# Batch 0 of a retention and gated-MLP kernel: the order of work on four engines, written anew

## The chip, the cores and the metric

The kernel runs on one core of a Trainium2 chip. A core has a matmul engine (PE, with weight loads as PEld), a vector engine (DVE), a scalar engine (ACT), GpSimd (POOL), and SyncE (SP), which here only issues DMA transfers. Each engine works through its own list of instructions in order and waits at an instruction until the semaphores it names have come. The metric is the device time of one execution in microseconds (us); lower is better.

## The reference, cut to what matters

```
scores = scale * (q @ k.T)                      # per batch (8) and head (8), 576 x 576
ret    = scores * gamma[h] ** (i - j), i >= j   # decay mask
x      = ret @ v                                # 576 x 512 per batch
h      = relu(x @ w_in);  u, v = h[:, :512], h[:, 512:]
v_n    = (v - mean) / sqrt(var + 1e-6)
v_s    = w_spatial @ v_n + b_spatial
out    = (u * v_s) @ w_out
```

All of it is in float32, for 8 batches.

## The kernel before, in words

Every large product is made of three fp32r matmuls on operands split into a rounded part (hi) and a remainder (lo): `mm3`. So each operand has to be split first: ACT writes hi, then DVE or POOL writes lo.

The **retention** of a batch b goes over the sequence in chunks c = 0 to 4, four of 128 rows and a tail of 64 (`NC` = 4).

- `scores(b, c)` puts a chunk's score matmuls into one of two PSUM banks, r_95 and r_96 (the two alternate); DVE multiplies by the mask into the tile `at`.
- `prep(b, c)` lets POOL scale k by `kd` (tile `qkv`) and q by `qs` (tile `qsc`).
- `burst(b, c, nx)` does on PE, in one run, the state products (need the scaled k), the product with the old state (needs the scaled q), the scores of the next chunk if one is given, and the product with `at`. Then DVE adds up the state `st` and POOL decays it.
- `evac(b, c)` copies the result out of PSUM: ACT writes hi and DVE lo, into `x`, for the tail into `xt`. The next burst uses the same bank and waits for it.
- `load(b, c)` has SP fetch a chunk's qkv (1024 KB) and q (256 KB). The qkv tiles have two buffers, so a load waits for the burst two chunks back.

The **MLP** of a batch has stages. `v_steps(b, sb)` is one row block of v in steps: matmuls, ACT's relu, DVE's statistics, ACT's square root and subtraction, the reciprocal chain on DVE (tile `sm`) and the split into `vn` (tail: `vt1`, `vt2`). `vs_mm` is one tile of w_spatial @ v_n: 12 matmuls 128x288 on `wsp` and `vn`, then one with `wtl[0]` and one with `wtl[1]`. `u_mm` is a tile of u, f is the output product.

The **weights** come as 8-byte words of which the kernel makes float32. `front(kind, i)` takes the absolute value on ACT and clamps it on POOL (tile `f`), `mid` is a DVE TENSOR_SCALAR and two SCALAR_TENSOR_TENSOR, `back` is the split into `win` or `wout` (ACT, then POOL). Kind 1 is the v half of w_in, kind 0 its u half, kind 2 is w_out; `fetch` loads block i of one. `w_sp_steps` splits w_spatial: four blocks, and in its fifth step the tail `wtl` with the row of b_spatial.

The steady part, batches 1 to 7 from v1 on, is ordered by a scheduler. Batch 0 and the retention of batch 1 are ordered by hand: while `ordered[0]` is true, each engine issues in the order in which the program's text calls it. `go(gen, n)` does the next n steps of such a generator; `ret` is the retention of batch 1, whose first `go` does the scores of chunk 0 and whose later ones a burst with its evac and its next load each. PSUM for all but the retention is four buffers in turn (`ps_m`).

Since one helper issues every ordered instruction, all have line L71 in the profile; tiles tell them apart.

Of the kernel before, what the change touches and what calls it, by code (L numbers as in the profile page):

```python
# [33 lines left out]
def retention_gmlp(ctx, tc, qkv, q_x, qk_t, q_xt, v_t, w_in, w_sp, b_sp, w_out, amask, qscale, kdec, sdec, out):  # L34
# [20 lines left out]
    def slot(name):  # L55
        return cp.tile([P, 2, NCB, S], F32R, name=name, tag="slot", bufs=2)
# [24 lines left out]
    def dma(dst, src):  # L81
        return sy.dma_start(out=dst, in_=src)
# [88 lines left out]
    for i in range(2, NCB):  # L171
        fetch(1, i)
    dma(sd, sdec)
    load(0, 1)
    dma(qs, qscale)
    load(0, 2)
    load(0, 3)
    load_qsc(0, NC)
# [9 lines left out]
    def front(kind, i, clamp=po):  # L188
        words = staged[kind, i].rearrange("p (n two) -> p n two", two=2)
        hw, lw = words[:, :, 1], words[:, :, 0]  # L190
        f = early[:, i] if kind == 1 else sp.tile([P, 512], F32, name=f"f_{kind}{i}", tag="f", bufs=3)
        a = f if clamp is po else ps_m.tile([P, 512], F32, name=f"w_{kind}{i}", tag="m")
        ac.activation(out=a, in_=hw.bitcast(F32), func=AF.Abs)
        if clamp is po:
            po.tensor_scalar(out=a, in0=a, scalar1=2.0 ** -15, scalar2=None, op0=ALU.max)
        part[kind, i] = hw, lw, a, f
# [27 lines left out]
    def w_sp_steps():  # L224
        w = staged["s"]
        for sb in range(NC):
            split(wsp[0][:, sb], wsp[1][:, sb], w[:, sb], po)
            yield
        t = w[:, NC]
        ac.copy(out=wtl[0], in_=t)  # L230
        po.tensor_tensor(out=wtl[1][:TL], in0=t[:TL], in1=wtl[0][:TL].bitcast(F32), op=ALU.subtract)
        r = slice(TL, TL + 1)
        t = w[r, NC + 1]
        ac.copy(out=wtl[1][r], in_=t)
        po.tensor_tensor(out=wtl[1][96:97], in0=t, in1=wtl[1][r].bitcast(F32), op=ALU.subtract)
        yield

    xs = {}
# [82 lines left out]
            po.tensor_copy(out=xs[b][:, :, :, t], in_=xt.rearrange("p a i n -> p i a n"))  # L321

    def retention(b):
        xs[b] = slot(f"x_{b}")
        nxt = [(b, c) for c in range(NC + 1)] + [(b + 1, c) for c in range(2)]
        if (b, 0) not in at:
            prep(b, 0)
            scores(b, 0)
        yield 0.95
        for c in range(NC + 1):  # L330
            nx = nxt[c + 1] if nxt[c + 1][0] < B and (b, c) != (1, NC) else None
            if nx:
# [12 lines left out]
    def v_steps(b, sb):  # L345
        n = C if sb < NC else TL
        x = xs[b]
        pf = ps_m.tile([P, 512], F32, name=f"v_{b}_{sb}", tag="m")
        ps = pf[:n]
        t = slice(sb * C, sb * C + n)  # L350
        if sb < NC:
            for cb in range(NCB):
                if cb == 2 and (b, sb) == (0, 3):
                    yield
                mm3(ps, [x[:, i, cb, t] for i in range(2)], [win[i][:, cb, DH:] for i in range(2)], cb == 0, cb == NCB - 1)
        else:
# [12 lines left out]
        mv = wk.tile([P, 2], F32, name=f"mv_{b}_{sb}", tag="mv", bufs=3)[:n]
        ve.bn_aggr(out=mv, in_=s6)  # L370
        s = wk.tile([P, 5], F32, name=f"sm_{b}_{sb}", tag="sm", bufs=3)[:n]
        ac.activation(out=s[:, 0:1], in_=mv[:, 1:2], func=AF.Sqrt, bias=eps[:n])
        ac.activation(out=ps, in_=ps, func=AF.Identity, scale=-1.0, bias=mv[:, 0:1])
        yield
        r = s[:, 1:2]
        ve.reciprocal(out=r, in_=s[:, 0:1])
        ve.tensor_scalar(out=s[:, 2:3], in0=mv[:, 1:2], scalar1=EPS, scalar2=r, op0=ALU.add, op1=ALU.mult)
        ve.tensor_scalar(out=s[:, 3:4], in0=s[:, 2:3], scalar1=r, scalar2=0.5, op0=ALU.mult, op1=ALU.mult)
        ve.tensor_scalar(out=s[:, 4:5], in0=s[:, 3:4], scalar1=-1.5, scalar2=r, op0=ALU.add, op1=ALU.mult)
        nrstd = s[:, 4:5]  # L380
        if sb < NC:
            hi, lo = vn[0][:, sb], vn[1][:, sb]
        else:
            hi, lo = vt1[:TL], vt1[TL:]
            ac.activation(out=vt2[:TL], in_=ps, func=AF.Copy, scale=nrstd)
        ac.activation(out=hi, in_=ps, func=AF.Copy, scale=nrstd)
        yield
        ve.scalar_tensor_tensor(out=lo, in0=ps, scalar=nrstd, in1=hi.bitcast(F32), op0=ALU.mult, op1=ALU.subtract)
        yield
# [85 lines left out]
    def go(gen, n=1):  # L475
        for _ in range(n):
            next(gen)
# [9 lines left out]
    front(1, 2, ve)  # L487
    back(1, 1)
    front(1, 3)
    burst(0, 0, None)  # L490
    mid(1, 2)
    evac(0, 0)
    load(0, NC)
    fetch(0, 0)
# [2 lines left out]
    scores(0, 1)  # L497
    back(1, 2)
    mid(1, 3)
    burst(0, 1, None)  # L500
    back(1, 3, ve)
    fetch_wsp()
    evac(0, 1)
    load(1, 0)
    for i in range(1, NDB):
        fetch(0, i)
    prep(0, 2)
    scores(0, 2)
    vn = [cp.tile([P, NC, DH], F32R, name=f"vn{i}", tag=f"vn{i}") for i in range(2)]
    v = [v_steps(0, sb) for sb in range(NC + 1)]  # L510
    m = [mid_steps(0, i) for i in range(NDB)]
    sps = w_sp_steps()

    go(v[0], 2)
    burst(0, 2, None)
    go(v[0])
    front(0, 0)
    evac(0, 2)
    prep(0, 3)
    scores(0, 3)  # L520
    go(v[0], 2)
    go(v[1], 2)
    burst(0, 3, None)
    go(v[1])
    go(m[0])
    evac(0, 3)
    prep(0, NC)
    scores(0, NC)
    go(v[1], 2)
    go(m[0])  # L530
    go(v[2], 2)
    burst(0, NC, None)
    go(sps, 2)
    load(1, 1)
    go(v[2])
    evac(0, NC)
    back(0, 0)
    go(v[3])
    go(v[4])
    go(v[3])  # L540
    go(v[2], 2)
    go(v[4])
    go(v[3])
    go(sps)
# [2 lines left out]
    for t in range(2):  # L547
        ps = ps_m.tile([P, 512], F32, name=f"u_0_0_{t}", tag="m")[:, :HALF]
        u_mm(0, 0, t, ps)
        ac.activation(out=pre[:, t, :HALF], in_=ps, func=AF.Relu)  # L550
    go(v[4])
    go(v[3])
    go(sps)
    go(v[3])
    go(v[4])
    go(v[3])
    go(sps)
    go(v[4])
# [4 lines left out]
    def u_work():
        for i in range(1, NDB):
            front(0, i)
            yield
            go(m[i])
            yield
            go(m[i])
            back(0, i)  # L570
            yield

    def wout_work():
        for i in range(NMB):
            fetch(2, i)
        for i in range(NMB):
            front(2, i)
            yield
            mid(2, i)
            yield  # L580
            back(2, i)
            yield

    work = u_work()
    for t in range(2):
        ts = slice(t * HALF, (t + 1) * HALF)
        for db in range(NDB):
            ps = vs_mm(0, db, t)
            if db:
                ac.copy(out=u[:, db, ts], in_=ps)  # L590
            else:
                ve.tensor_tensor(out=u[:, db, ts], in0=ps, in1=pre[:, t, :HALF], op=ALU.mult)
            next(work, None)
            if (t, db) in ((0, 2), (1, 1)):
                go(ret)
            next(work, None)
    for _ in work:
        pass
    wout = [cp.tile([P, NDB, DM], F32R, name=f"wout{i}", tag=f"wout{i}") for i in range(2)]
    work = wout_work()  # L600
    g0 = xs[0]
    for t in range(2):
        ts = slice(t * HALF, (t + 1) * HALF)
        for db in range(1, NDB):
            ps = ps_m.tile([P, 512], F32, name=f"u_0_{db}_{t}", tag="m")[:, :HALF]
            u_mm(0, db, t, ps)
            ve.scalar_tensor_tensor(out=u[:, db, ts], in0=ps, scalar=0.0, in1=u[:, db, ts], op0=ALU.max, op1=ALU.mult)
            next(work)
            if db == 2:
                go(ret)  # L610
        split(g0[:, 0, :, ts], g0[:, 1, :, ts], u[:, :, ts], po)
    ordered[0] = False
    for eng in (pe, ve, ac, po):
        ctx.enter_context(tc.issue_after(eng.last))
# [85 lines left out]
```

## Time and profile before

| | us |
|---|---|
| time, median of 3 runs (range) | 570.96 (570.17 to 571.62) |
| the profiled execution: its own time | 569.64 |
| its span, first to last instruction | 567.9 |
| PE busy in the span | 539.2 |
| PE busy in 0 to 122 us | 96.43 |
| PE busy in 122 to 568 us | 442.74 |
| DVE, ACT, POOL busy in the span | 266.1, 207.2, 132.7 |

Batch 0's stages are the first 122 us. In a timeline row the columns are start, duration, engine, line, operation, output and inputs, shape, count, and in brackets the idle time ahead of the row with what ended it. Neighbouring rows of one kind are merged, so a duration can cover many instructions. In a row of a table by stretches stand the stretch, its length, the busy time (and count) of PE, PEld, DVE, ACT and POOL, the granted PE clock (1.00 is full), the DMA share and GB/s.

### The profile page before, as it was taken

To read this page: it belongs to the slowest core of one execution; us is meant where nothing else is said; L and a number is where in the kernel's file an instruction comes from. 1 tells how busy PE (TensorE), PEld (TensorE's weight loads), DVE (VectorE), ACT (ScalarE), POOL (GpSimd) and SP (SyncE) were. 2 spreads that over 40 slices of the span, in tenths; PEclk is the share of its full clock that TensorE was granted. 3 is DMA by queue.
4 is the path that set the end of the run, shared out by engine and by line. 5 is a ranking of instruction groups with operands and counts; after the bars stand their busy time and mean duration, and the time that the engine had idled before them with its cause. 6 is when DMAs were issued, how large, how long until landed. Compare 5 with 4: busy or idle time off the path is not lost.

```text
span 567.9 us, 15304 instructions
## 1 busy us (share of the span) xinstructions
PE 539.2 (95%) x6735; PEld 501.3 (88%) x6735; DVE 266.1 (47%) x588; ACT 207.2 (36%) x445; POOL 132.7 (23%) x131
## 2 busy tenths in 40 slices
PE   6885689899999999999999999999999999999997
PEld 5764689789999899998999899998999889998997
DVE  5855445480463473417353373516543383515340
ACT  4237221582212462226422362225522362225422
POOL 4635554670031220121201221021201212000000
PEclk8889789899999999999999999999999999999999
DMA  8972228301346421342224441342213432010002
GB/s 326 377 236 86 92 96 266 115 1 42 117 125 192 171 95 47 105 166 76 95 48 145 138 156 48 95 169 83 95 47 126 145 104 88 27 64 21 2 1 84
DMA packets 37045, 64.08 MB, mean 113 GB/s; under 512 B 14833, under 2 KB 27249, under 8 KB 33010
## 3 DMA queue, kind: packets, MB, share of 16 engines
q1 hardware_dynamic: 36978, 63.10, 33.7%
q8 instruction: 53, 0.87, 0.7%
q14 instruction: 14, 0.11, 0.1%
HBM read 53.65 MB, written 9.44 MB: 111 GB/s over the span
## 4 chain that ended last, share of the span: by engine, by line
PE 84%; POOL 5%; DVE 4%; DMA 3%; ACT 2%; issue 1%; SPq 0%; POOLq 0%; ACTq 0%; DVEq 0%
PE vs L71 20%; PE f L71 18%; PE u L71 17%; PE v L71 15%; PE r L71 14%; POOL f L71 2%; DVE f L71 2%; DMA qs<-in_qscale 2%; DMA am<-in_amask 1%; POOL x L71 1%; POOL qsc L71 1%; POOL qkv L71 1%; DVE st L71 1%; ACT x L71 1%; DVE at L71 0%
## 5 line engine op out<-in xcount | busy, mean ns | idle before, releaser
L71 PE MATMUL vs<-wsp,vn 128*128 128x288 f32 x768 | 114.1, 297 | 0.0
L71 PE MATMUL u<-x,win 128*128 128x288 f32 x768 | 106.6, 298 | 1.0 <-POOL f L71 1.0
L71 PEld LDWEIGHTS vs<-wsp,vn 128*128 128x128 f32 x768 | 105.2, 188 | 1.2
L71 PEld LDWEIGHTS u<-x,win 128*128 128x128 f32 x768 | 104.2, 190 | 2.3 <-POOL f L71 1.2
L71 PE MATMUL v<-win,x 128*128 128x512 f32 x384 | 94.1, 400 | 0.0
L71 PE MATMUL f<-g,wout 128*128 128x288 f32 x672 | 92.3, 296 | 0.0
L71 PEld LDWEIGHTS f<-g,wout 128*128 128x128 f32 x672 | 89.8, 188 | 0.5
L71 DVE TENSOR_TENSOR at<-r,am 128x1024 f32<-128x1024 f32 (+1 forms) x40 | 44.5, 1112 | 93.4 <-PE r L71 93.4
L71 PEld LDWEIGHTS v<-win,x 128*128 128x128 f32 x384 | 71.8, 190 | 16.8
L71 POOL TENSOR_TENSOR qsc<-qsc,qs 128x512 f32<-128x512 f32 (+1 forms) x31 | 36.3, 1171 | 175.8 <-DMA qsc<-in_q_x 99.6
L71 PEld LDWEIGHTS r<-qkv 64*64 64x64 f32 x2176 | 48.4, 141 | 25.8 <-POOL qkv L71 15.3
L71 PE MATMUL r<-qkv 64*64 64x64 f32 (+1 forms) x2176 | 54.9, 242 | 17.0 <-POOL qkv L71 13.1
L71 DVE BATCH_NORM_STATS2 s<-v 128x6 f32<-128x512 f32 (+1 forms) x40 | 27.8, 694 | 59.4 <-ACT v L71 58.4
L71 ACT COPY o<-f 128x288 f32<-128x288 f32 x64 | 25.6, 400 | 72.0 <-PE f L71 71.9
L71 ACT CAST g<-vs 128x288 fp32r<-128x288 f32 x56 | 22.3, 399 | 75.8 <-DVE vs L71 74.7
L71 POOL TENSOR_TENSOR qkv<-qkv,kd 128x512 f32<-128x512 f32 x32 | 33.3, 1044 | 41.6 <-DMA qkv<-in_qkv 27.3
L71 ACT CAST x<-r 128x512 fp32r<-128x512 f32 x32 | 18.7, 585 | 60.7 <-DVE st L71 60.7
L71 PE MATMUL r<-at,qkv 64*64 64x64 f32 (+1 forms) x1152 | 38.8, 232 | 0.0
L71 DVE TENSOR_TENSOR g<-vs,g 128x288 fp32r<-128x288 f32 x56 | 25.6, 457 | 26.3 <-ACT g L71 26.3
L71 DVE TENSOR_TENSOR vs<-vs,u 128x288 f32<-128x288 f32 x56 | 26.0, 464 | 23.1 <-PE vs L71 23.0
L71 PEld LDWEIGHTS r<-at,qkv 64*64 64x64 f32 (+1 forms) x1152 | 33.2, 145 | 2.5 <-DVE at L71 0.2
L71 POOL TENSOR_TENSOR st<-st,sd 128x256 f32<-128x256 f32 x24 | 14.7, 614 | 87.2 <-DVE st L71 87.2
(73 smaller groups left out, 504.5 us busy)
## 6 DMA issues: line engine op xcount, KB each, us to landing
qkv<-in_qkv SPq DMA_DIRECT2D x31, 1024.0 KB, 5.7
out<-o SPq DMA_DIRECT2D x64, 144.0 KB, 1.8
qsc<-in_q_x SPq DMA_DIRECT2D x24, 256.0 KB, 3.2
raw_v<-in_w_in SPq DMA_DIRECT2D x4, 512.0 KB, 6.3
qkv<-in_qk_t SPq DMA_DIRECT2D x8, 256.0 KB, 3.4
qkv<-in_v_t SPq DMA_DIRECT2D x16, 128.0 KB, 3.1
raw<-in_w_in SPq DMA_DIRECT2D x4, 512.0 KB, 8.6
raw<-in_w_out SPq DMA_DIRECT2D x4, 512.0 KB, 7.3
```

The costliest lines, as they stand in the source:

```text
L71: ins = op(*args, **kw)
```

## The change

Only text between the start of the kernel and the line `ordered[0] = False` is different. The stages come in the same order (v0, vs0, u0, v1, u1, f0), and the number of matmuls, casts and transfers is the same, except that the split of the gated result goes in halves (`split_g`, two ACT casts and two POOL subtractions for one each). The core of the diff:

```diff
+    dma(qs, qscale)
     load(0, 1)
-    dma(qs, qscale)
...
+    mid(1, 2)
     burst(0, 0, None)
-    mid(1, 2)
     evac(0, 0)
...
     mid(1, 3)
-    burst(0, 1, None)
     back(1, 3, ve)
     fetch_wsp()
+    burst(0, 1, None)
+    prep(0, 2)
     evac(0, 1)
...
-    go(v[0], 2)
+    go(v[0], 3)
+    prep(0, 3)
     burst(0, 2, None)
+    evac(0, 2)
     go(v[0])
     front(0, 0)
-    evac(0, 2)
-    prep(0, 3)
     scores(0, 3)
-    go(v[0], 2)
-    go(v[1], 2)
+    go(v[0])
+    go(v[1], 3)
+    prep(0, NC)
     burst(0, 3, None)
-    go(v[1])
     go(m[0])
     evac(0, 3)
-    prep(0, NC)
+    go(v[1])
     scores(0, NC)
-    go(v[1], 2)
-    go(m[0])
+    go(v[1])
+    go(sps, 2)
     go(v[2], 2)
     burst(0, NC, None)
-    go(sps, 2)
+    evac(0, NC)
+    go(v[2])
+    go(m[0])
+    back(0, 0)
     load(1, 1)
-    go(v[2])
-    evac(0, NC)
-    back(0, 0)
+    fetch(2, 0)
+    prep(1, 0)
+    go(sps)
     go(v[3])
     go(v[4])
     go(v[3])
     go(v[2], 2)
     go(v[4])
     go(v[3])
     go(sps)
+    ret = retention(1)
+    xs[1] = slot("x_1")
+    scores(1, 0)
+    go(v[4])
+    go(v[3])
+    go(sps)
...
         ac.activation(out=pre[:, t, :HALF], in_=ps, func=AF.Relu)
+        go(v[4 - t])
     go(v[4])
     go(v[3])
...
-    ret = retention(1)
-    go(ret)
     go(ret)
+    vs_tile(0, 0)
+    go(ret)
+    front(0, 1)
+    vs_tile(0, 1)
+    front(0, 2)
+    vs_tile(0, 2)
+    go(m[1], 2)
+    vs_tile(0, 3)
+    back(0, 1)
+    front(0, 3)
+    fetch(2, 1)
+    go(ret)
+    vs_tile(1, 0)
+    go(m[2], 2)
+    vs_tile(1, 1)
+    back(0, 2)
+    fetch(2, 2)
+    vs_tile(1, 2)
+    go(ret)
+    go(m[3], 2)
+    vs_tile(1, 3)
+    back(0, 3)
+    fetch(2, 3)
+    front(2, 0)
+    gated_u(0, 1)
+    gated_u(0, 2)
+    front(2, 1)
+    go(ret)
+    mid(2, 0)
+    gated_u(0, 3)
+    back(2, 0)
+    split_g(0)
+    gated_u(1, 1)
+    gated_u(1, 2)
+    go(ret)
+    mid(2, 1)
+    gated_u(1, 3)
+    back(2, 1)
+    split_g(1)
...
```

Left out at the dots are, above all, the old form of the lower half: six more steps of v[3], v[4] and sps ahead of the retention, and two loops that took the same vs and u tiles with `front`, `mid` and `back` of w_in's blocks 1 to 3 and of w_out one step after each tile. There all four `fetch(2, i)` stood together, between the vs tiles and the u tiles. `vs_tile`, `gated_u` and `split_g` are the bodies of those loops, given names.

In the last step of `w_sp_steps` the row of b_spatial now goes ahead of the tail of w_spatial, and in `v_steps` of the tail `vt1` ahead of `vt2`.

How this moves instructions on the engines is shown at three places. In the rows, the last number of a name is an instance number; `qkv_3_133` is chunk 3's tile.

POOL, after the state decay of chunk 1 of batch 0, before:

```order
L71 TENSOR_TENSOR qsc_2_131<-qsc_2_131,qs 128x512
L71 TENSOR_TENSOR st_88<-st_87,sd 128x256
L71 TENSOR_SCALAR f_409<-f_409 128x512
L71 TENSOR_TENSOR qkv_3_133<-qkv_3_133,kd 128x512
L71 TENSOR_TENSOR qsc_3_135<-qsc_3_135,qs 128x512
L71 TENSOR_TENSOR qkv_2_129<-qkv_2_129,qs 128x256
```

and changed:

```order
L71 TENSOR_TENSOR qsc_2_131<-qsc_2_131,qs 128x512
L71 TENSOR_TENSOR qkv_3_133<-qkv_3_133,kd 128x512
L71 TENSOR_TENSOR qsc_3_135<-qsc_3_135,qs 128x512
L71 TENSOR_TENSOR st_88<-st_87,sd 128x256
L71 TENSOR_SCALAR f_418<-f_418 128x512
L71 TENSOR_TENSOR qkv_2_129<-qkv_2_129,qs 128x256
```

The two scalings of chunk 3 (rows with qkv_3 and qsc_3) now stand ahead of the state decay and of the clamp of weight block 0 (f).

POOL further on, at the split of w_spatial, before (qkv_0_315 and qkv_1_559 are chunks 0 and 1 of batch 1):

```order
L71 TENSOR_TENSOR win_78<-f_409,win_77 128x4x128
L71 TENSOR_TENSOR wsp_80<-raw_s,wsp_79 128x576 x2
L71 TENSOR_TENSOR wtl_82<-raw_s,wtl_81 64x576
L71 TENSOR_TENSOR wtl_82<-raw_s,wtl_82 1x576
L71 TENSOR_TENSOR qkv_0_315<-qkv_0_315,kd 128x512
L71 TENSOR_TENSOR qkv_1_559<-qkv_1_559,kd 128x512
```

and changed (qkv_0_317 and qkv_1_571):

```order
L71 TENSOR_TENSOR win_78<-f_418,win_77 128x4x128
L71 TENSOR_TENSOR qkv_0_317<-qkv_0_317,kd 128x512
L71 TENSOR_TENSOR wsp_80<-raw_s,wsp_79 128x576 x2
L71 TENSOR_TENSOR wtl_82<-raw_s,wtl_82 1x576
L71 TENSOR_TENSOR wtl_82<-raw_s,wtl_81 64x576
L71 TENSOR_TENSOR qkv_1_571<-qkv_1_571,kd 128x512
```

The scaling of batch 1's chunk 0 now stands ahead of the last four splits. On PE the scores of that chunk now come before the two u tiles, and its burst after the first vs tile instead of before it.

DVE in the vs stage, before (f_770 and f_794 are weight blocks 1 and 2, at_2 and x belong to batch 1):

```order
L71 TENSOR_SCALAR f_770<-f_770 128x512
L71 SCALAR_TENSOR_TENSOR f_770<-raw_317,f_770 128x512 x2
L71 TENSOR_SCALAR f_794<-f_794 128x512
L71 SCALAR_TENSOR_TENSOR f_794<-raw_319,f_794 128x512
L71 TENSOR_TENSOR at_2_857<-r_96,am 128x1024
L71 TENSOR_TENSOR st_88<-r_95,st_88 128x256
L71 TENSOR_TENSOR st_86<-r_95,st_88 128x256
L71 TENSOR_TENSOR x_673<-r_95,x_673 128x2x2x128
```

and changed (f_772 and f_791):

```order
L71 TENSOR_SCALAR f_772<-f_772 128x512
L71 SCALAR_TENSOR_TENSOR f_772<-raw_319,f_772 128x512 x2
L71 TENSOR_TENSOR at_2_878<-r_96,am 128x1024
L71 TENSOR_TENSOR st_88<-r_95,st_88 128x256
L71 TENSOR_TENSOR st_86<-r_95,st_88 128x256
L71 TENSOR_TENSOR x_615<-r_95,x_615 128x2x2x128
L71 TENSOR_TENSOR u<-vs_0_1_905,pre 128x288
L71 TENSOR_SCALAR f_791<-f_791 128x512
L71 SCALAR_TENSOR_TENSOR f_791<-raw_321,f_791 128x512 x2
```

Weight block 2 (f_794, now f_791) has moved from ahead of at_2 to behind the x that frees the bank. The same was done at chunk 4, where w_out's first block stood ahead of at_4.

From v1 on the lists of PE and SP are the same rows in the same order; on ACT, DVE and POOL a few neighbours have changed places.

More of the change, by code (lines that the diff above doesn't have):

```diff
@@ L228, in w_sp_steps @@
             yield
-        t = w[:, NC]
-        ac.copy(out=wtl[0], in_=t)
-        po.tensor_tensor(out=wtl[1][:TL], in0=t[:TL], in1=wtl[0][:TL].bitcast(F32), op=ALU.subtract)
         r = slice(TL, TL + 1)
@@ L235, in w_sp_steps @@
         po.tensor_tensor(out=wtl[1][96:97], in0=t, in1=wtl[1][r].bitcast(F32), op=ALU.subtract)
+        t = w[:, NC]
+        ac.copy(out=wtl[0], in_=t)
+        po.tensor_tensor(out=wtl[1][:TL], in0=t[:TL], in1=wtl[0][:TL].bitcast(F32), op=ALU.subtract)
         yield
@@ L323, in retention @@
     def retention(b):
-        xs[b] = slot(f"x_{b}")
+        if b not in xs:
+            xs[b] = slot(f"x_{b}")
         nxt = [(b, c) for c in range(NC + 1)] + [(b + 1, c) for c in range(2)]
@@ L384, in v_steps @@
             hi, lo = vt1[:TL], vt1[TL:]
+        ac.activation(out=hi, in_=ps, func=AF.Copy, scale=nrstd)
+        if sb == NC:
             ac.activation(out=vt2[:TL], in_=ps, func=AF.Copy, scale=nrstd)
-        ac.activation(out=hi, in_=ps, func=AF.Copy, scale=nrstd)
         yield
@@ L506, in retention_gmlp @@
         fetch(0, i)
-    prep(0, 2)
     scores(0, 2)
@@ L550, in retention_gmlp, with vs_tile, gated_u, split_g @@
         ac.activation(out=pre[:, t, :HALF], in_=ps, func=AF.Relu)
+        go(v[4 - t])
     go(v[4])
     go(v[3])
[L553 to L558, printed above, removed]
-    ret = retention(1)
-    go(ret)
-    go(ret)
[L563 to L571, printed above, removed]
+    go(ret)
+    def vs_tile(t, db):
+        ts = slice(t * HALF, (t + 1) * HALF)
+        ps = vs_mm(0, db, t)
+        if db:
+            ac.copy(out=u[:, db, ts], in_=ps)
+        else:
+            ve.tensor_tensor(out=u[:, db, ts], in0=ps, in1=pre[:, t, :HALF], op=ALU.mult)
+    def gated_u(t, db):
+        ts = slice(t * HALF, (t + 1) * HALF)
+        ps = ps_m.tile([P, 512], F32, name=f"u_0_{db}_{t}", tag="m")[:, :HALF]
+        u_mm(0, db, t, ps)
+        ve.scalar_tensor_tensor(out=u[:, db, ts], in0=ps, scalar=0.0, in1=u[:, db, ts], op0=ALU.max, op1=ALU.mult)
+    def split_g(t):
+        ts = slice(t * HALF, (t + 1) * HALF)
+        for db in range(0, NDB, 2):
+            ds = slice(db, db + 2)
+            split(xs[0][:, 0, ds, ts], xs[0][:, 1, ds, ts], u[:, ds, ts], po)
+    vs_tile(0, 0)
+    go(ret)
+    front(0, 1)
[19 more added lines that the diff above has]
+    fetch(2, 3)
+    wout = [cp.tile([P, NDB, DM], F32R, name=f"wout{i}", tag=f"wout{i}") for i in range(2)]
+    front(2, 0)
[14 more added lines that the diff above has]
+    split_g(1)
     def wout_work():
-        for i in range(NMB):
-            fetch(2, i)
-        for i in range(NMB):
+        for i in range(2, NMB):
             front(2, i)
@@ L582, in wout_work @@
             yield
[L584 to L594, printed above, removed]
-                go(ret)
[L596 to L599, printed above, removed]
     work = wout_work()
     g0 = xs[0]
[L602 to L611, printed above, removed]
     ordered[0] = False
```

## The prediction

> **What bounds the kernel now.** I began with the page's first line and PE's busy row, then asked for two stretches, batch 0's part and the rest:
>
> ```profile
> span 567.9 us, 15304 instructions
> PE 539.2 (95%) x6735; PEld 501.3 (88%) x6735; DVE 266.1 (47%) x588; ACT 207.2 (36%) x445; POOL 132.7 (23%) x131
> 0.00:122.00 122.00, 96.43 (x1309) 83.41 (x1310) 71.58 (x145) 50.34 (x96) 67.65 (x61) 0.90 0.54 186
> 122.00:568.00 446.00, 442.74 (x5428) 417.85 (x5427) 194.56 (x444) 156.81 (x350) 65.02 (x70) 1.00 0.29 93
> ```
>
> PE is the bound. After 122 us it stands still for 3.3 us of 446; before that for 25.6 of 122, and there its granted clock is 0.90. The change touches only those 122 us, so the question is how much of the 25.6 us and of the slow clock it removes. PE's timeline shows where they lie:
>
> ```profile
> 27.49 3.07 PE L71 MATMUL v<-win,x 128*128 128x512 f32 x12
> 32.64 0.69 PE L71 MATMUL r<-qkv 64*64 64x64 f32 x32 [2.08 <-POOL qkv L71]
> 36.64 3.56 PE L71 MATMUL v<-win,x 128*128 128x512 f32 x12
> 46.11 2.11 PE L71 MATMUL v<-win,xt 128*128 128x512 f32 x8 [3.39 <-DVE xt L71]
> 48.06 1.56 PE L71 MATMUL v<-win,x 128*128 128x512 f32 x6
> 49.46 3.35 PE L71 MATMUL u<-x,win 128*128 128x288 f32 x24
> 61.88 2.41 PE L71 MATMUL r<-qkv 64*64 64x64 f32 x64 [8.25 <-POOL qkv L71]
> 65.44 1.86 PE L71 MATMUL vs<-wsp,vn 128*128 128x288 f32 x12
> 67.41 1.76 PE L71 MATMUL vs<-wsp,vn 128*128 128x288 f32 x12
> 81.49 0.69 PE L71 MATMUL r<-qkv 64*64 64x64 f32 x32 [1.84 <-DVE x L71]
> 101.79 0.46 PE L71 MATMUL r<-qsc,st 64*64 64x64 f32 x16 [1.88 <-DVE x L71]
> 105.32 11.67 PE L71 MATMUL v<-win,x 128*128 128x512 f32 x48
> ```
>
> A wait costs more than its length. Behind three of these restarts the granted clock (the third number from the end) falls to half, while PE is busy:
>
> ```profile
> 35.00:37.50 2.50, 2.50 (x36) 2.17 (x35) 1.27 (x3) 0.00 (x0) 0.00 (x0) 0.50 1.09 350
> 82.00:82.50 0.50, 0.50 (x27) 0.50 (x20) 0.00 (x0) 0.50 (x1) 0.00 (x0) 0.64 0.00 0
> 85.50:86.00 0.50, 0.50 (x8) 0.41 (x5) 0.47 (x2) 0.00 (x0) 0.00 (x0) 0.95 0.00 0
> 102.50:105.00 2.50, 2.50 (x11) 2.50 (x12) 0.24 (x1) 1.53 (x3) 2.02 (x2) 0.52 0.54 138
> 42.50:45.00 2.50, 0.22 (x1) 0.00 (x0) 1.89 (x4) 1.90 (x5) 1.64 (x2) 1.00 0.81 331
> ```
>
> In the two half-us rows the fall comes at 82.14 and the return at 85.55 (0.64 and 0.95 as mixtures of 1 and 0.5): 3.4 us at half speed, a loss of 1.7 us, after a wait of 1.84. The last row shows that a wait need not do it: during the 3.39 us ahead of 46.11 the clock stayed at 1.00.
>
> **The change, part by part.** Behind each wait stands an instruction that was ready but queued behind one that was not:
>
> ```profile
> 30.09 1.49 POOL L71 TENSOR_SCALAR f<-f 128x512 f32<-128x512 f32 x1 [1.67 <-ACT f L71]
> 31.55 1.04 POOL L71 TENSOR_TENSOR qkv<-qkv,kd 128x512 f32<-128x512 f32 x1
> 42.62 1.23 ACT L71 CAST wsp<-raw_s 128x576 fp32r<-128x576 f32 x2
> 44.45 0.29 ACT L71 ACTIVATE sm<-mv,eps 128x1 f32<-128x1 f32 x1 [0.60 <-DVE mv L71]
> 45.23 0.37 ACT L71 CAST xt<-r 128x256 fp32r<-128x256 f32 x1
> 55.94 0.75 DVE L71 SCALAR_TENSOR_TENSOR vn<-v,sm,vn 128x512 fp32r<-128x512 f32 x1
> 55.95 1.25 ACT L71 ACTIVATE vt<-v,sm 64x512 fp32r<-64x512 f32 x2
> 57.10 1.35 ACT L71 CAST wtl<-raw_s 128x576 fp32r<-128x576 f32 x2
> 60.79 2.04 POOL L71 TENSOR_TENSOR qkv<-qkv,kd 128x512 f32<-128x512 f32 x2
> 75.06 1.26 DVE L71 TENSOR_SCALAR f<-f 128x512 int32<-128x512 int32 x1 [3.50 <-POOL f L71]
> 77.95 1.21 DVE L71 TENSOR_TENSOR at<-r,am 128x1024 f32<-128x1024 f32 x1
> 96.46 0.95 DVE L71 TENSOR_SCALAR f<-f 128x512 int32<-128x512 int32 x1 [3.18 <-POOL f L71]
> ```
>
> *Term 1, chunk 3's scaled k.* POOL waited 1.67 us for ACT's f and clamped for 1.49 before it scaled chunk 3. Now both scalings stand ahead of the clamp, right behind chunk 2's, while PE is still in chunk 2's burst and in v1 (24.54 to 30.56). From v1's end (27.49 + 3.07 = 30.56) to v2's start (36.64) lay 6.1 us. The same burst at full clock takes 2.1 us (24.54 to 26.66 for chunk 2, row below), plus 0.3 for the tail's scores: 2.4. That gives 3.7; v2 itself at full clock saves 0.5 (3.56 against 3.07); I take off 0.2 because `back(1, 3, ve)` now holds DVE's state of chunk 1 up by that. Gain 4.0, between 2.0 (the wait alone) and 4.2.
>
> *Term 2, the tail's xt.* ACT's xt stood behind the two wsp casts and behind v2's square root with its 0.60 wait and the subtraction after it. The wsp casts stay ahead of it; the root, the wait and the subtraction (44.45 less 43.85, to 45.23: 1.4 us) go behind. ACT also comes to v1's vn about 1 us sooner against PE, since v1's reciprocal chain now stands ahead of at_4 on DVE. Of 3.39 some 0.9 is left: gain 2.5, between 1.4 and 3.4.
>
> *Term 3, from v3's end to the second vs tile.* This stretch ran from 49.6 (48.06 + 1.56) to 67.41, 17.8 us: two u tiles, scores, 8.25 of waiting, a burst at half clock, the first vs tile. The wait came from POOL's kd for batch 1's chunk 0 (60.79), queued behind wtl. Now kd is done early and the burst goes behind the first vs tile, so vn of v3 and wtl are late next. Before, vn's lo part ended 56.69, 7.1 us after v3. To that chain are added at_0 on DVE (1.2), and wtl (1.35) and vt (1.25) that now go ahead of vn on ACT; a wait for the second u tile (1.2) and a wsp cast (0.66) drop out: 9.0. The first nine matmuls of the vs tile need only blocks 0 to 2 and run inside that time; 0.45 remains (three of 0.15, from 1.76 for 12), then a burst without the old state, 2.2. PE still idles for some 4 us here, so I add half of a slow stretch, 0.8. New length 12.4 or 12.5; gain 5.4, between 3.0 (vn 2.5 us later) and 7.2 (no slow clock, a chain 0.9 shorter).
>
> *Term 4, the vs and u stage.* At 75.06 DVE waited 3.50 us for POOL's clamp of weight block 2, with at_2 queued behind it (77.95), then the state and x; so x was late and PE waited 1.84. At 96.46 the same with w_out's first block, whose transfer was issued only at 88.50: 1.88. In the new order block 2 comes after x, and w_out's block 0 is fetched ahead of batch 1's chunk 2 and used after chunk 4's burst is issued. at_2 and at_4 then start as their scores end. Removed: 3.7 us of waiting and the two slow stretches, 3.4 of loss. Gain 7.1, between 2.0 (each wait half gone, both slow stretches still there) and 7.1.
>
> Costed at nothing: qscale's transfer ahead of chunk 1's, because POOL needs qscale and both tiles of chunk 1 and the last of the three keeps its place in the queue:
>
> ```profile
> 8.89 8.92 DMA qs<-in_qscale
> 24.54 0.69 PE L71 MATMUL r<-qkv 64*64 64x64 f32 x32
> 26.66 0.90 PE L71 MATMUL r<-qkv 64*64 64x128 f32 x32
> 65.61 0.33 SPq L71 DMA_DIRECT2D qkv<-in_qkv  x1
> 88.50 2.28 SPq L71 DMA_DIRECT2D raw<-in_w_out  x4
> qkv<-in_qkv SPq DMA_DIRECT2D x31, 1024.0 KB, 5.7
> ```
>
> If chunk 1 itself came 1.4 us later, its scores would lose the cover of the spin matmuls: 1 us either way. The split in halves and the moved ACT copies are covered by PE's u tiles (24 of them 3.35 us).
>
> The sum is 4.0 + 2.5 + 5.4 + 7.1 = 19.0 us. This walk lets every instruction start when it is ready. Three places in term 4 have margins of 1 to 1.5 us only (two qkv loads, below, and the split of block 3 for its u tile). I set one short wait of 0.2 with a slow stretch of 1.7 against them: 17.1. The profiled execution took 569.64 (span 567.9); it would take 552.5. The runs' median is 1.3 above it: 570.96 - 17.1 = 553.9.
>
> [...]
>
> **The rivals.** *A, loads behind weights:* SP now has `fetch(2, 1)` and `fetch(2, 2)` between the qkv loads, and each waits until DVE has read an old weight block. A load is issued as its burst ends (65.61) and lands 5.7 us later by the page's median; its scores come three vs tiles (1.97 for one, 65.44 to 67.41: 5.9) and two parts of a burst behind. A w_out block of 512 KB ahead adds 1.5 at the 331 GB/s of the last clock row. If chunks 2 and 3 are each 1 us late and each wait draws a slow stretch, 5.4 is lost: 19.0 - 5.4 = 13.6, 557.4. For it: the margin; against it: the w_out blocks are ready before the bursts end.
>
> *B, DVE and POOL in each other's way:* the TENSOR_SCALAR of 75.06 ran 1.26 us beside a POOL instruction that started first; its like at 69.68 took 0.43:
>
> ```profile
> 69.68 0.43 DVE L71 TENSOR_SCALAR f<-f 128x512 int32<-128x512 int32 x1 [1.21 <-POOL f L71]
> ```
>
> The new order lays more such pairs side by side. Three delays of 0.8 on the vn chain, and one wait with a slow stretch in the vs stage, 2.7: 19.0 - 5.1 = 13.9, 557.1. [...]
>
> *C, the change doesn't do what it says:* the two waits of term 4 and their slow stretches come back at other bursts, because POOL's clamps still queue ahead of the scalings of chunks 2 and 3; without term 4 and with term 3 at its low end, 9.5 is left: 561.5.
>
> *D, slower:* the fetches block SP. `fetch(2, 1)` waits for weight block 1's `mid`, which waits for POOL's clamp, which stands behind the state decay of the burst just issued; load, burst and decay then follow each other in a ring. It decides once the three loads come 6.3 us late each (19.0 / 3); at 7.5 the time is 574.5. Against it: block 1's clamp is issued a whole burst earlier than its load's buffer comes free.
>
> **How the numbers follow.** Forecast 0.62, A 0.18, B 0.10, C 0.06, D 0.04. The predicted time is 553.9. Its own low end is the full 19.0 with 1 us from the start and another for short waits not counted: 549.9. Up to 561 the range holds A and B and nearly C. Differences under 0.3% (1.7 us) can't be told from none. Faster by more: 0.95; slower: D less its mild half, 0.03; the same, 0.02.
>
> **What would show it.** The PE waits for POOL qkv at 2.08 and 8.25 us are gone (terms 1, 3); ahead of v's tail under 1.5 us is left (2); one wait of 2 to 5 us inside or ahead of the first vs tile, ended by DVE or ACT vn (3); between it and v1 no wait over 0.5 us, and no row at clock 0.50 (4); v1 begins near 88 us instead of 105.3. A PE wait ended by a qkv transfer shows A, DVE rows over 1 us for a TENSOR_SCALAR before such a wait B. A second stretch of 10 us with PE under 80% busy after 55 us would make the sum wrong.

## The result and the profile after

The changed kernel takes 555.27 us (median of 4 runs, 554.89 to 555.73) where the kernel before took 571.29 on the same chip (4 runs, 570.17 to 571.67): a ratio of 0.972, interval 0.971 to 0.974, or 16.0 us. The prediction said 17.1 less and 553.9. The profiled execution took 555.62, with a span of 553.7; against the profiled one of before that is 14.0 less, since that one lay 1.65 us under 571.29 and the changed one 0.35 over 555.27. What follows explains the 14.0.

PE's busy row on the page after, and the two stretches (columns as before: stretch, length, busy time of PE, PEld, DVE, ACT and POOL, granted clock, DMA share, GB/s):

```profile
PE 536.8 (97%) x6735; PEld 498.0 (90%) x6735; DVE 269.0 (49%) x588; ACT 207.4 (37%) x447; POOL 133.9 (24%) x133
0.00:122.00 122.00, 108.17 (x1416) 94.24 (x1417) 79.89 (x158) 56.93 (x112) 71.73 (x65) 0.94 0.54 186
122.00:553.70 431.70, 428.59 (x5321) 403.73 (x5320) 189.15 (x430) 150.42 (x335) 62.13 (x68) 1.00 0.30 96
```

In the first 122 us PE now stands still for 13.8 us instead of 25.6, at a granted clock of 0.94 instead of 0.90. The rest is as it was. PE's timeline after, with all its waits from v1 of batch 0 on:

```profile
26.11 0.67 PE L71 MATMUL r<-qsc,st 64*64 64x128 f32 x16 [0.54 <-POOL qsc L71]
28.38 3.07 PE L71 MATMUL v<-win,x 128*128 128x512 f32 x12
33.68 3.06 PE L71 MATMUL v<-win,x 128*128 128x512 f32 x12
37.58 0.46 PE L71 MATMUL r<-at,qkv 64*64 64x64 f32 x16 [0.45 <-DVE at L71]
40.14 2.11 PE L71 MATMUL v<-win,xt 128*128 128x512 f32 x8 [0.51 <-DVE xt L71]
42.09 1.56 PE L71 MATMUL v<-win,x 128*128 128x512 f32 x6
44.41 3.45 PE L71 MATMUL u<-x,win 128*128 128x288 f32 x24
50.28 1.46 PE L71 MATMUL vs<-wsp,vn 128*128 128x288 f32 x9 [2.42 <-ACT pre L71]
52.29 1.40 PE L71 MATMUL vs<-wsp,vn 128*128 128x288 f32 x3 [0.54 <-ACT vn L71]
54.09 2.41 PE L71 MATMUL r<-qkv 64*64 64x64 f32 x64
57.91 2.20 PE L71 MATMUL vs<-wsp,vn 128*128 128x288 f32 x12
73.93 0.90 PE L71 MATMUL r<-qkv 64*64 64x128 f32 x32 [0.41 <-DMA qkv<-in_qkv]
90.28 11.36 PE L71 MATMUL v<-win,x 128*128 128x512 f32 x48
107.45 11.52 PE L71 MATMUL u<-x,win 128*128 128x288 f32 x84 [2.24 <-ACT u L71]
118.81 12.87 PE L71 MATMUL f<-x,wout 128*128 128x288 f32 x96
```

The waits of 2.08, 8.25, 1.84 and 1.88 us are gone and that of 3.39 is 0.51. New are 2.42 us at the first vs tile (50.28) and 2.24 us in batch 1's u stage (107.45, 0.99 before). The first was forecast in size, but as a wait for `vn`; the row has it ended by `pre`, into which ACT writes the first u tile out of PSUM. The second was not forecast. The clock around 50.28, in three stretches of 3.41 us of which the second begins where it falls and the third ends where it returns, and PE's share around 107.45:

```profile
48.44:51.85 3.41, 1.46 (x9) 1.22 (x9) 1.13 (x5) 3.36 (x8) 2.42 (x2) 1.00 0.01 2
51.85:55.26 3.41, 2.97 (x45) 2.41 (x49) 1.50 (x3) 0.39 (x1) 2.63 (x3) 0.50 0.00 0
55.26:58.68 3.42, 3.42 (x67) 3.19 (x60) 1.47 (x2) 0.37 (x1) 0.00 (x0) 0.50 0.02 5
100.00:110.00 10.00, 7.76 (x47) 6.68 (x46) 9.72 (x23) 6.79 (x15) 7.80 (x6) 1.00 0.00 0
```

The second and third rows, 51.85 to 58.68, are 6.83 us at half clock, in which the last rows of the vs tile and the whole burst of batch 1's chunk 0 run. The prediction had put in half of a 3.4 us stretch.

Place by place, in the terms of the prediction. Up to v2's end (36.74 against 40.20) 3.5 us are won; to the start of v's tail (40.14 against 46.11) 2.5 more. From v3's end (43.65) to the second vs tile (57.91) it takes 14.3 us where it took 17.8: 3.5. From there to v1 of batch 1 (90.28) 32.4 where it took 37.9: 5.5. From v1 to f, 28.5 us where before it was 27.6 (105.32 to 132.96): 0.9 lost. Sum 14.1.

### The profile page after: what moved, and what is told of

It is laid out like the page before. It is cut to its first block, busy times and chain, and to the rows that moved or that the text cites. A ratio compares the mean times of both kernels' runs of the same rounds, so it can differ in the third digit from the quotient of the medians.

```text
span 553.7 us, 15312 instructions
## 1 busy us (share of the span) xinstructions
PE 536.8 (97%) x6735; PEld 498.0 (90%) x6735; DVE 269.0 (49%) x588; ACT 207.4 (37%) x447; POOL 133.9 (24%) x133
## 4 chain that ended last, share of the span: by engine, by line
PE 85%; DMA 5%; DVE 5%; ACT 3%; issue 1%; POOL 1%; SPq 0%; ACTq 0%; DVEq 0%
PE vs L71 21%; PE f L71 19%; PE u L71 17%; PE v L71 14%; PE r L71 14%; DMA qkv<-in_qkv 5%; DVE f L71 2%; DVE s L71 1%; ACT x L71 1%; DVE sm L71 1%; ACT vn L71 0%; POOL qsc L71 0%; DVE vn L71 0%; DVE w L71 0%; POOL qkv L71 0%
## 5 line engine op out<-in xcount | busy, mean ns | idle before, releaser
L71 PE MATMUL vs<-wsp,vn 128*128 128x288 f32 x768 | 115.6, 299 | 3.0 <-ACT pre L71 2.4
L71 PEld LDWEIGHTS u<-x,win 128*128 128x128 f32 x768 | 103.0, 188 | 3.7 <-POOL f L71 2.5
L71 ACT COPY o<-f 128x288 f32<-128x288 f32 x64 | 25.6, 400 | 72.0 <-PE f L71 71.9
L71 DVE TENSOR_TENSOR g<-vs,g 128x288 fp32r<-128x288 f32 x56 | 25.6, 458 | 26.3 <-ACT g L71 26.3
L71 PE MATMUL r<-at,qkv 64*64 64x64 f32 (+1 forms) x1152 | 37.6, 228 | 0.4 <-DVE at L71 0.4
```

The costliest lines, as they stand in the source:

```text
L71: ins = op(*args, **kw)
```

## The experiments

Theory: each of the four parts pays as its term says, and what is missing is one slow stretch behind the first vs tile. The rivals are given with each run. The runs came in three groups, and the medians of the kernel before on the same chips were 571.19, 570.97 and 570.82. The changed kernel's 555.27 was measured ahead of them; a later run of the very same instruction lists, below, gave 555.43. Single runs of one kernel lie 0.3 to 6 us apart, so a term under 1 us is read from a trace.

**Chunk 3's scaling put back behind the clamp (term 1 undone).**

```diff
-    prep(0, 3)
     burst(0, 2, None)
     evac(0, 2)
     go(v[0])
     front(0, 0)
+    prep(0, 3)
```

> The changed kernel with chunk 3's two scalings on POOL put back behind the clamp of weight block 0. Theory (term 1): ACT's absolute value comes at 32.2, the clamp ends 33.8, so the scaled q is ready at 36 instead of 28.3 and the burst that started at 31.4 ends 4 us later, with a slow stretch on top at times: 4 to 6 us slower than the change, 559 to 561. Rival (later waits absorb it, since v's tail and vn are set by ACT and DVE): under 1.5 us slower.

Measured 559.81 (559.60 to 559.94), 4.5 slower than the changed kernel. PE waits, and restarts at half clock (timeline and stretches of this kernel):

```profile
35.38 1.14 PE L71 MATMUL r<-qkv 64*64 64x64 f32 x32 [3.39 <-POOL qkv L71]
31.83:35.24 3.41, 0.16 (x1) 0.00 (x0) 2.23 (x4) 2.24 (x5) 2.41 (x2) 1.00 1.01 362
35.24:38.66 3.42, 3.20 (x74) 2.89 (x76) 0.00 (x0) 0.00 (x0) 1.99 (x3) 0.50 0.81 259
```

Term 1 holds with the rest of the change in place.

**Term 1 alone, in the kernel before.**

```diff
     go(v[0], 2)
+    prep(0, 3)
     burst(0, 2, None)
     ...
-    prep(0, 3)
```

> The kernel before, with chunk 3's scaling of k moved ahead of burst(0, 2) and nothing else. Theory (term 1 stands alone): the 2.08 us wait for POOL qkv at 32.64 goes, v2 follows v1 by 2.4 to 3 us in place of 6.1, and the run is 2 to 4 us faster than the kernel before, about 568 against 571. Rival (the gain is eaten by the wait for xt ahead of v's tail, which is set by ACT and not by PE): that wait grows from 3.39 to 5.5 to 7, v's tail begins near 46 as before, and the run is within 0.7 of the kernel before.

Measured 569.78 against 570.82: a ratio of 0.998, interval 0.995 to 1.000, so 1.0 us. Neither is right. Timeline and clock of this kernel:

```profile
29.78 3.06 PE L71 MATMUL v<-win,x 128*128 128x512 f32 x12
36.09 3.06 PE L71 MATMUL v<-win,x 128*128 128x512 f32 x12
40.92 0.46 PE L71 MATMUL r<-qkv,st 64*64 64x64 f32 x16 [1.76 <-DVE x L71]
46.87 2.09 PE L71 MATMUL v<-win,xt 128*128 128x512 f32 x8 [2.13 <-DVE xt L71]
42.50:45.00 2.50, 2.23 (x6) 1.22 (x4) 1.97 (x4) 2.11 (x4) 0.89 (x1) 0.50 0.82 246
```

From v1's end to v2 it takes 3.25 us instead of 6.1, so 2.8 are won there. But the tail's burst now waits 1.76 us for `evac`'s x, and the clock falls behind it: from v1's start to the tail 17.1 us instead of 18.6, a gain of 1.5. The rest of the 3.5 then has to come from the moved `evac` and `go` lines around it, which no run moves by themselves. The terms of a sum like this one aren't additive one by one.

**The tail's xt put back behind v2's root and subtraction (term 2 undone).**

```diff
-    evac(0, NC)
     go(v[2])
+    evac(0, NC)
```

> The changed kernel with the tail's evacuation (ACT's and DVE's xt) put back behind v2's statistics, square root and subtraction. Theory (term 2): xt's lo part ends near 41.9 instead of 40.1, v's tail starts 1.8 us later, and all behind it: 1.5 to 3 us slower, 557 to 558. Rival (hidden behind the chain to vn): same as the change within 0.5 us.

Measured 556.89 (555.54 to 558.49), 1.6 slower by the medians; the fastest of the four lies among the changed kernel's runs. The profiled one was the slowest. In it the wait at the tail is back, and the tail runs slowly:

```profile
42.30 3.23 PE L71 MATMUL v<-win,xt 128*128 128x512 f32 x8 [2.34 <-DVE xt L71]
```

**Term 3, its two halves.** One kernel puts the scaling of batch 1's chunk 0 back behind the splits of w_spatial, one puts its burst back ahead of the first vs tile, and one does both.

```diff
     fetch(2, 0)
-    prep(1, 0)          # scaling late
     go(sps)
     ...
     go(v[3])
+    prep(1, 0)
     go(ret)
     ...
-    vs_tile(0, 0)       # burst first
     go(ret)
+    vs_tile(0, 0)
```

Scaling late alone:

> The changed kernel with only the scaling of batch 1's chunk 0 on POOL moved back behind the splits of w_spatial; the first vs tile stays ahead of the burst. Theory: the scaling then ends near 53.3, and the burst started only at 54.1, behind the vs tile, so nothing changes: within 0.5 us of the change. Rival (the early scaling is what removed the 8.25 us wait): 2 to 5 us slower than the change.

Burst first alone:

> The changed kernel with batch 1's first burst put back ahead of the first vs tile; its scaled k stays early (POOL, 43.7 us). Theory: the scaled k and the scores are ready when the second u tile ends (47.9), so the burst fills PE's 2.4 us wait, the clock stays full, and only the last three matmuls of the first vs tile wait for vn (53.0): the second vs tile starts near 53.5 instead of 57.9, 4.4 us faster than the change, about 551. Rival (the new place of the burst is what shortened this stretch): the burst ahead costs as before, 2 us slower than the change or more, 557 or above.

Both:

> The changed kernel with both undone: scaling behind the splits and burst ahead of the first vs tile, as before the change. Theory: the burst waits for the scaling until 53.3, runs at half clock to about 57, and the vs tile follows to about 59.5: some 2 us slower than the change, 557 to 558, which is what the order of this stretch alone is worth. Rival (term 3 as predicted, 5.4): 5 us slower, 560 or above.

Measured 554.38, 552.62 (550.77 to 554.04) and 557.94. With the burst first and the scaling early, PE's timeline is

```profile
51.21 1.46 PE L71 MATMUL vs<-wsp,vn 128*128 128x288 f32 x9 [0.30 <-ACT pre L71]
53.21 0.53 PE L71 MATMUL vs<-wsp,vn 128*128 128x288 f32 x2 [0.55 <-ACT vn L71]
54.00 0.40 PE L71 MATMUL vs<-wsp,vn 128*128 128x288 f32 x1 [0.26 <-DVE vn L71]
54.50 1.75 PE L71 MATMUL vs<-wsp,vn 128*128 128x288 f32 x12
```

and with both undone

```profile
52.77 2.41 PE L71 MATMUL r<-qkv 64*64 64x64 f32 x64 [5.43 <-POOL qkv L71]
```

So the early scaling is what allows the gain (552.62 against 557.94 with the burst first), and moving the burst behind the first vs tile gave part of it away: ahead of it, the burst fills the time in which PE waits. From v3's end to the second vs tile it takes 9.9 us with the burst first (44.57 to 54.50) and 14.3 in the changed kernel's profile. The chain to vn's lo sets when the first vs tile can end in either order; what stands behind that tile is added to it. With the burst late, no difference by the place of the scaling can be told (554.38 against 555.27, ranges overlapping), and the burst does not wait for POOL. With both undone a wait of 5.43 us is back, where it was 8.25 before the change, and the stretch takes 15.3 us (43.13 to 58.45) instead of 17.8. So 2.5 us of the term come from the rest of the order, which no run takes apart; by the medians the two moves undone cost 2.7.

**Ten idle matmuls ahead of the first vs tile**, to keep PE busy through the wait; they write to a bank that is free.

```diff
+    ps = banks[1].rearrange("p i n -> p (i n)")[:, :512]
+    for i in range(10):
+        pe.matmul(ps, idle[:, :P], idle, start=True, stop=True)
     go(v[4])
```

> The changed kernel with ten idle matmuls 128x512 into a free PSUM bank between the second u tile and the first vs tile, in PE's wait. They take 2.3 us at full clock and use no buffer that anything waits for. Theory: the slow clock from 51.9 to 58.7 comes from that wait; with it filled the burst runs in 2.2 instead of 3.8 us and the second vs tile starts 2.2 to 2.7 us earlier: about 552.8. Rival (the clock is not the reason, the burst waits for data): same as the change, or slower by the spin's own time.

Measured 553.45 (553.21 to 555.99), 1.8 less than the changed kernel. In its timeline the idle matmuls end as the inputs come, and burst and next vs tile run at full clock:

```profile
47.05 2.47 PE L71 MATMUL r<-wsp 128*128 128x512 f32 x10
53.02 1.36 PE L71 MATMUL r<-qkv 64*64 64x64 f32 x64
55.16 1.87 PE L71 MATMUL vs<-wsp,vn 128*128 128x288 f32 x12
```

From the start of the u tiles (43.76) to the second vs tile 11.4 us, 13.5 in the changed kernel's profile: the slow stretch costs 2.1. This one trace doesn't show that the idle matmuls removed the stretch: the second profile of the changed kernel's lists, below, takes 11.4 us too (45.08 to 56.50), without them. For them speak the medians and three of the four runs, which lie below all of the changed kernel's. The edit has a second effect: the scheduler gave DVE and ACT another order around batch 1's u stage, and from v1 to f it takes 29.5 us here, 28.5 in the changed kernel's profile.

**Weight block 2 put back ahead of at_2 (part of term 4 undone).**

```diff
-    front(0, 2)
     vs_tile(0, 2)
     ...
     back(0, 1)
+    front(0, 2)
     front(0, 3)
     fetch(2, 1)
+    go(m[2])
     go(ret)
     vs_tile(1, 0)
-    go(m[2], 2)
+    go(m[2])
```

> The changed kernel with weight block 2's absolute value, clamp and first two DVE steps put back ahead of batch 1's chunk 2 mask (the old place, behind block 1's split). Theory (half of term 4): the clamp ends near 68, at_2 starts near 69.4 instead of 65.9, x near 72.2, and the burst at 72.4 waits 0.5 to 1.8 us, with a slow stretch of up to 1.7: 0.5 to 3.5 us slower. Rival (the order on DVE did not matter, the earlier start of the stage did): same within 0.4 us.

Measured 555.11 (553.53 to 556.73), the same as the changed kernel, as the rival had it. One wait came,

```profile
73.21 0.69 PE L71 MATMUL r<-qkv 64*64 64x64 f32 x32 [0.47 <-DVE x L71]
```

but of 0.47 us, not 1.84, and no row behind it was below full clock. The late clamp is not the difference: DVE waits for it here too, 4.40 us against 3.50 in the kernel before. The difference is how long DVE took over the weight rows between the clamp and at_2. One of them in the kernel before, then one of this run:

```profile
76.35 1.67 DVE L71 SCALAR_TENSOR_TENSOR f<-raw,f 128x512 int32<-128x512 int32 x1
68.19 0.82 DVE L71 TENSOR_SCALAR f<-f 128x512 int32<-128x512 int32 x1 [4.40 <-POOL f L71]
```

From the clamp's end to the start of at_2 it took 2.9 us in the kernel before (75.06 to 77.95) and takes 1.5 here (68.19 to 69.66); these 1.4 us are the difference of the two waits. In the kernel before the two DVE rows ran beside POOL's two scalings (74.98 to 77.48), here beside a clamp. So the place in DVE's list alone does not cost the 1.84; with it went slow DVE rows beside POOL's scalings, as in rival B, before the change already. That POOL's work is what slowed them is argued from the rows and not shown by a run. No run undoes the rest of term 4, the place and the earlier fetch of w_out's first block, so what removed its second wait is read from the traces alone.

**The two fetches behind the following load of qkv** (rival A, in which weights hold up loads).

```diff
-    fetch(2, 1)
     go(ret)
+    fetch(2, 1)
     ...
-    fetch(2, 2)
     vs_tile(1, 2)
     go(ret)
+    fetch(2, 2)
```

> The changed kernel with the fetches of w_out blocks 1 and 2 issued behind the qkv load that follows them instead of ahead. Theory (rival A of the prediction came true in small): PE's 0.41 us wait for chunk 3's qkv at 73.9 goes: 0.3 to 0.6 us faster. Rival: the load is late by its own buffer, not by the weights: same, within 0.2.

Measured 554.65 (552.03 to 555.89). The 0.41 wait for DMA qkv is gone and v1 starts at 89.48 instead of 90.28; the medians (0.6 apart) can't tell it. Nor does the trace settle it: with the fetches ahead, the wait is missing in the second profile of the changed kernel's lists, where chunk 3's load landed 5.5 us after its issue instead of 7.1, and in the profiles of six more of the kernels here; the idle-matmul kernel has one of 0.39, at chunk 2. So a load for which PE waits does come at times, at a tenth of rival A's price; that the weights ahead of it are the reason is not shown.

**The 2.24 us wait in batch 1's u stage.** Rows of DVE and ACT in the changed kernel:

```profile
103.61 1.48 DVE L71 TENSOR_SCALAR f<-f 128x512 int32<-128x512 int32 x1
105.20 0.90 DVE L71 SCALAR_TENSOR_TENSOR f<-raw,f 128x512 int32<-128x512 int32 x1
106.15 0.20 DVE L71 TENSOR_SCALAR sm<-mv,sm 128x1 f32<-128x1 f32 x1
106.32 0.69 ACT L71 ACTIVATE vn<-v,sm 128x512 fp32r<-128x512 f32 x1 [1.18 <-DVE sm L71]
106.90 0.40 ACT L71 ACTIVATE u<-u 128x288 f32<-128x288 f32 x1
```

A weight block of w_out now stands on DVE inside v's reciprocal chain (in the kernel before it came behind vn, 0.42 us at 122.17 in its trace), it takes 1.48 us beside a POOL instruction, and vn, u and PE follow. I tried to take this block out of the v stage:

```diff
-    for stage in (v_stage(1), u_stage(1)):
-        for _ in stage:
-            next(work, None)
+    for _ in v_stage(1):
+        pass
+    for _ in u_stage(1):
+        next(work, None)
```

> Weight blocks 2 and 3 of w_out are split during batch 1's u stage alone, no longer during its v stage. Theory (the 2.24 us that PE waits for ACT u at 107.45 after the change is the v stage's vn chain held up on DVE, GpSimd and ACT by this splitting): the wait falls to about 1 us or less, the f stage starts 1 to 2 us earlier (118.81 to about 117.3), the run is near 554.0 against 555.3. Rival (the wait belongs to the order of the two stages itself, as the 0.99 us ahead of the change shows): the wait stays near 2.2 and the time at 555.3. Third case: six split steps in the u stage's 13 us come too late, the f stage waits for wout on DVE or ACT by 1 to 4 us, 556 to 559.

The edit did nothing: here the scheduler sets the order, and it gave every engine the same list as in the changed kernel. Measured 555.43 (554.43 to 556.45), the wait 2.23. So the cause of this wait is read from the rows above, and no run tests it.

The run is worth something all the same, as a second look at the very same lists. Its timeline and clock:

```profile
42.76 1.56 PE L71 MATMUL v<-win,x 128*128 128x512 f32 x6
50.96 1.46 PE L71 MATMUL vs<-wsp,vn 128*128 128x288 f32 x9 [2.43 <-ACT pre L71]
56.50 1.86 PE L71 MATMUL vs<-wsp,vn 128*128 128x288 f32 x12
87.89 11.36 PE L71 MATMUL v<-win,x 128*128 128x512 f32 x48
105.04 12.87 PE L71 MATMUL u<-x,win 128*128 128x288 f32 x84 [2.23 <-ACT u L71]
46.92:50.33 3.41, 1.61 (x13) 1.37 (x11) 2.71 (x12) 3.06 (x7) 1.73 (x2) 1.00 0.00 0
50.33:53.74 3.41, 1.99 (x11) 1.52 (x11) 1.49 (x2) 2.59 (x6) 3.33 (x3) 1.00 0.01 2
105.00:107.50 2.50, 2.46 (x10) 2.49 (x11) 2.50 (x6) 1.09 (x3) 1.36 (x1) 0.50 0.00 0
```

The same wait at the first vs tile (2.43 and 2.42) was followed by full clock, and the same wait in the u stage (2.23 and 2.24) by half clock, the other way round than in the first profile. From v3's end to the second vs tile it took 12.2 us (44.32 to 56.50) instead of 14.3; the u stage took 12.87 instead of 11.52. So the slow stretch behind the first vs tile costs 2.1 us or nothing, that in the u stage 1.35 or nothing, in executions of one and the same order. The two don't add up to the scatter of single runs: in all seven profiles with the burst late and no idle matmuls exactly one of the two, that burst or the u stage, runs at half clock, so that together they part two runs by about 1 us. The kernel's start scatters as well: v0 begins at 21.75 in the first profile and at 23.29 in the second, where the clock was still at half until 23.02.

**A version that beats both**: the burst ahead of the first vs tile, and the fetches behind the loads. Its diff is that of the two runs above together.

> The changed kernel with the burst of batch 1's chunk 0 ahead of the first vs tile and the two weight blocks fetched behind the following qkv load. If the two gains add (2.65 by the medians of the first alone, 0.6 of the second): 552.0 against 555.3, no PE wait over 0.6 us between 50 us and v1, v1 near 85. [...]

Measured 551.22 (550.10 to 552.28), a ratio of 0.965 to the kernel before, interval 0.962 to 0.967. v1 begins at 85.03, as expected, but the ranges of this version and of the burst first alone (550.77 to 554.04) overlap, so it isn't shown that the moved fetches add anything. A run that was to add the edit of the u stage,

> The kernel of the run before with w_out's blocks 2 and 3 split during batch 1's u stage alone. If the wait of 2.24 us ahead of batch 1's u stage comes from that splitting, about 550.8, 1 to 1.5 below that run; if not, the same as that run; if the f stage now waits for wout, 1 to 4 above it.

is, for the reason above, the same lists again: 551.52 (550.17 to 553.69). Over the ten runs of both the median is 551.4, 3.9 us under the changed kernel. v1 of this version, and the one long wait left:

```profile
85.03 11.36 PE L71 MATMUL v<-win,x 128*128 128x512 f32 x48
102.17 11.53 PE L71 MATMUL u<-x,win 128*128 128x288 f32 x84 [2.25 <-ACT u L71]
```

## Why the prediction was right, and where it was off

The sign, the four places and their order of size held, and the time came out 1.4 us over the forecast. That it came so close is in part luck: the discount of 1.9 was meant for short waits in term 4 and met other losses, and between the two profiled executions, on whose rows the terms stand, the gain is 14.0 us and not 17.1. Point by point:

- **Term 1** (4.0; measured 3.5). The stretch behind v1 shrank to 2.23 us, forecast 2.4, and v2 ran at full clock. Off was what `back(1, 3, ve)` costs DVE's state of chunk 1: I took 0.2, and it came 0.9 later than before (22.26 against 21.35). With it POOL's scalings began late, PE waited 0.54 at 26.11, and v1 began 0.9 later than before. In the second profile, where v0 itself began later, that wait is not there. By the two runs the term is worth 4.5 undone and 1.0 alone, so it stands, but not by itself.
- **Term 2** (2.5; measured 2.5, and 1.6 by the run that undoes it). Of the wait 0.51 was left, and 0.45 at 37.58, together near the 0.9 that I had counted.
- **Term 3** (5.4; measured 3.5 in the first profile, 5.6 in the second). The chain to vn's lo was forecast at 9.0 us behind v3. Here is its last step in the changed kernel:

```profile
52.27 0.75 DVE L71 SCALAR_TENSOR_TENSOR vn<-v,sm,vn 128x512 fp32r<-128x512 f32 x1
```

It ends at 53.02, 9.4 us behind v3's end. Wrong was that the first nine matmuls of the vs tile need only blocks 0 to 2: they waited 2.42 us for `pre` on ACT. That cost nothing by itself, since they still ended (51.74) ahead of vn. The mis-sized step is the slow stretch: 0.8 was put in as half of a 1.7 loss, and it costs 2.1 or nothing; that it goes from run to run is shown by two profiles of the same lists.
- **Term 4** (7.1; measured 5.5, and 6.5 in the second profile, 56.50 to 87.89). Both waits and both slow stretches are gone. Of the 1.6 that lack, 1.0 is missing in the first profile alone: 0.6 around the 0.41 wait for a load, and 0.3 in the first of these vs tiles, still at half clock (2.20 against 1.86 us). Of the other 0.6, 0.3 was counted in the wrong place, since the second slow stretch before the change reached into v1 of batch 1 (11.67 us, 11.36 after). The last 0.3 is not accounted for. Why at_2 was late the prediction had in part wrong: the queue order alone is worth 0.47 us of wait, as the run with block 2 put back shows, and the rest of the 1.84 came with slow DVE rows.
- **After v1** I forecast nothing. There 0.9 us went lost (2.24 of waiting against 0.99, less the 0.3 by which v1 ran shorter), and 2.2 in the second profile (29.9 us from v1 to f): the term that the sum lacked. The chain is rival B's (a DVE row over 1 us before a PE wait), at a place where the diff changes no line: the scheduler ordered the stage anew.
- **The discount** of 1.9 was set against short waits in term 4. More was lost, and mostly elsewhere: of the 19.0, 3.0 by the medians, and 4.9 in the first profile (0.5 in term 1, 1.9 in term 3, 1.6 in term 4, 0.9 after v1).
- **Rivals C and D** did not come: no PE wait of 1.8 us came back in the vs stage, and the only wait for a load there was 0.41.
- **What would show it.** The waits named for terms 1 to 3 went as said: those of 2.08 and 8.25 us are gone, and 0.51 is left ahead of v's tail. The new one at the first vs tile came with 2.42 us, but ended by ACT's `pre`, with only 0.54 more for vn. No wait over 0.5 us lies between the first vs tile and v1. Two signs failed in the first profile: rows at clock 0.50 behind the first vs tile, and v1 at 90.28 instead of near 88 (87.89 in the second). The sign that the sum would be wrong did show: a stretch of 10 us after 55 us with PE at 7.76.

What I missed altogether is that the diff's own order is not the best at its dearest place. I forecast some 4 us of idle PE ahead of the last three matmuls of the first vs tile, with the burst behind it, and never asked what those 4 us could be filled with. The burst was ready: the early scaling had seen to that.

## What to carry to other kernels

When a late operand is moved up, look at once for which ready work on the bounding engine can now stand inside the next wait; here that was worth 2.65 us more by the medians. A wait of PE had two prices here, its length and a slow stretch behind it, and the second was paid in one execution and not in another of the same lists (2.1 us or nothing behind 2.42 and 2.43 at the first vs tile), so plan for waits that are short or filled. And where a scheduler follows an order written by hand, an edit ahead of it may reorder what follows, while an edit in it may do nothing: compare the engines' lists first.

## What the runs showed of the hardware

Waits of the same length went with both clocks: 3.39 us ahead of v's tail in the kernel before left it at 1.00; 3.39 us in the kernel with chunk 3's scaling late took it to 0.50. In the trace of the kernel before all changes of the clock lie whole multiples of 3.41 us apart (from 20 us to 545 us at 34.35, 37.76, 58.24, 65.07, 82.14, 85.55, 102.62 and 106.03), and so they do in the changed kernel's (51.85 and 58.68). Two stretches of that grid in the kernel before:

```profile
41.18:44.59 3.41, 1.54 (x6) 0.92 (x6) 2.35 (x5) 2.46 (x5) 1.23 (x1) 1.00 0.70 226
44.59:48.00 3.41, 1.89 (x8) 1.59 (x9) 1.45 (x6) 2.21 (x5) 3.41 (x4) 1.00 0.40 159
```

They share the wait of 3.39 us: PE is idle for 1.87 us in one and 1.52 in the other, and the clock stays up. With chunk 3's scaling late, 3.25 us of idle PE lie in one stretch (31.83 to 35.24), and the clock falls at its end. At the first vs tile the changed kernel has 1.95 us in one stretch (48.44 to 51.85) and falls; its second profile has 1.80 and 1.42 (46.92 to 53.74, counted back by 3.41 us from its fall at 104.94) and doesn't. From 20 us to 545 us of the traces of the kernel before and of the changed one, the clock falls behind the three stretches at full clock with the most idle PE (3.41, 2.23 and 1.95 us) and behind none with 1.52 or less; of the three between, it falls behind those of 1.84 and 1.88 and not behind that of 1.87. So in these traces the falls went with the idle time within one stretch and not with the length of the wait: the 2.42 and 2.43 us at the first vs tile lay differently across the grid. With the ten idle matmuls PE is idle for 0.92 us in all of 47.5 to 57.5, and the clock stays at 1.00, which speaks for them too.

Not expected was that the slow time of the changed kernel lasts 6.83 us, two stretches, with PE idle for only 0.44 us of the first. In the kernel before the clock was back after one stretch of 3.41 us from 34.35, 82.14 and 102.62, with PE busy all through, and in the kernel with term 1 alone a slow stretch with 0.54 us of idle PE (41.86 to 45.27) was enough. The burst's matmuls of 64x64 are not the reason by themselves: in the kernel with chunk 3's scaling late such a burst filled the slow stretch from 35.24 to 38.66, and the clock was back behind it. What decides stays open.

The same DVE instruction, the TENSOR_SCALAR on f, takes 0.42 us in the changed kernel at 78.24, with POOL idle, and up to 1.48 us, at 103.61 beside POOL's work.
